# Expert counting for two tiles at a time, and the z chain on 128 rows

## The chip, the cores and the metric

The kernel runs on one core of one Trainium2 chip. Five engines work side by side, each through its own queue in order: TensorE (PE, with its weight loads shown as PEld), VectorE (DVE), ScalarE (ACT), GpSimd (POOL) and SyncE (SP), which here only starts DMAs. The metric is device time in microseconds, lower is better: 367.92 us before the change, the median of 3 runs (367.91 to 368.16).

## The reference

One input x (2048 tokens of 512 numbers) goes through two branches, mixed by a gate:

```python
pq = q @ w_phi; pk = k @ w_phi                       # 32 heads of 16
phi = concat(softmax(p), softmax(-p))                # 32 features a head
kv = sum_s phi_k * v;  z = sum_s phi_k
a = ((phi_q @ kv) / (phi_q @ z + 1e-6)) @ wo         # linear attention
s1, s2 = x @ w_q @ k1, x @ w_q @ k2                  # 32 heads, 16 scores each
e = 16 * argmax(s1) + argmax(s2)                     # one of 256 experts a head
b = sum_h gelu(x @ u[e_h]) * v[e_h]                  # g of a single choice is 1
out = sigmoid(x @ gate_w) * a + (1 - sigmoid(x @ gate_w)) * b
```

The second branch needs, for each token, how many of the 32 heads chose each of the 256 experts: b is (count * gelu(x @ u.T)) @ v.

## The kernel before

The tokens are 16 tiles of 128. Every f32 operand of a large product is split into a high part and a rest (names ending in h and l), and a product takes three matmuls: high by high, high by low, low by high. A first stage builds phi_k, kv and z over all 16 tiles and folds the score weights (tiles sh, sl). The second stage, from L801 on, is a pipeline over tiles that is written out by hand: every engine's queue holds its instructions in the order in which the program issues them. In iteration a it works on tile n = a+1 (scores, L847 to L861, and the choice of the best score, `best`), tile a (attention softmax, `soft_in` to `soft_b`), b = a-1 (phi turned by a DMA transpose, `planes` and `join`; the coefficients, `coef` and `c_planes`), z = a-2 (attention numerator, `mid_num`, and its tile c, `c_join`, `back_cl`) and y = a-3 (output product po, `push` and `pop`, with the rest of the numerator, `num_lo`).

TensorE's order in an iteration is: front_q(a) (bank pq), po(y), the mask of tile a (mk, `mid_mask`), oT(z), the scores s0(n) and s1(n), then pp(n). The 18 matmuls of po(y) are 8 with xh, then 6 with c (the last two with its low part cl), then 4 with xl.

The choice: DVE takes the maximum of 16 scores (L515) and marks the places that equal it (L516, tile eq); when both halves are marked, SP starts a DMA transpose of eq into et (`turn_eq`, L525), and TensorE multiplies et by powers of two in mk (L580): each head's choice becomes one bit in a 16-bit word. This mk stands in PE's queue ahead of the rest of the next iteration.

The counting (`count`, L585) is a chain of 17 small DVE instructions on 16-bit and 32-bit words, in 16 steps: four shifted ORs (L593 to L596), two XORs in one step (L600, L602), an AND into a table X (L613), then the usual bit sums (L616 to L624) and an addition of bytes into cf (L627). It is a generator: `step(t)` issues its next instruction, so its instructions are dealt out between the other work of DVE. Four ORs of tile a go into `soft_b(a)`, the other steps of tile b into the softmax of the next iteration (`dealt`, L785); tile 15, the last, is counted early, one or two steps an iteration. The softmax ends in four short DVE instructions (L494 to L500) and a multiplication on POOL (L507, two halves). POOL also computes w = phi * z (L479), `gelu_in` (L441), `gelu_out` (L451) and `coef` (L631).

The z chain runs once, in iteration 0: z lies in 8 columns; its high and low parts make a tile of 128 x 16 (`z_split`), which is transposed to 16 rows (`z_rows`, L744), multiplied by a selector (L748), and spread to all partitions by two matmuls with 16 rows (`z_spread`, L755).

## Time and profile before

| what | value |
|---|---|
| median of 3 runs | 367.92 us |
| time of the profiled execution | 368.09 us |
| its span, from the first to the last instruction | 366.3 us |
| TensorE busy | 361.1 us, 99% of the span |
| VectorE busy | 313.2 us, 86%, 729 instructions |
| ScalarE busy | 239.7 us, 65% |
| GpSimd busy | 159.9 us, 44% |
| granted TensorE clock | 1.00 |

A row of the timeline reads: start in us from the span's beginning, duration in us, engine, line, operation, output<-input, shapes, and in brackets the idle time before it and what ended it. Consecutive like instructions are merged into one row, and "x2" is their number. Instructions of one engine overlap at their ends, so the distance of two starts, not the duration, is what an instruction costs in a queue that never idles. A group row (out<-in xcount | busy, mean ns of one | idle before) sums all instructions of one line and shape.

### The profile page before, as it was taken

What the parts mean: (1) busy time and instruction counts of PE and PEld (TensorE: products, weight loads), DVE (VectorE), ACT (ScalarE), POOL (GpSimd) and SP (SyncE); (2) the same over time, 40 slices, a digit from 0 to 9 for tenths busy, and PEclk for the clock granted to TensorE, in tenths of its full rate; (3) what the DMA queues carried; (4) which work ended last, traced back from release to release, by engine and by line L of the source; (5) the groups of instructions that cost most, each with busy time, mean ns of one, the idle gap of its engine ahead of it and who ended that gap; (6) DMA issues with size and microseconds to landing.
All of it is one profiled execution on the core that took longest, in us unless ns stands there. A gap on an engine that the chain in (4) does not pass through costs nothing.

```text
span 366.3 us, 8798 instructions
## 1 busy us (share of the span) xinstructions
PE 361.1 (99%) x3512; PEld 289.9 (79%) x3512; DVE 313.2 (86%) x729; ACT 239.7 (65%) x440; POOL 159.9 (44%) x171
## 2 busy tenths in 40 slices
PE   8999999999999999999999999999999999999995
PEld 3767787787777888878888888888888888888874
DVE  2459898866759979989999999999999999999883
ACT  4444557636538555778687596696786876968552
POOL 2204365525323833627245364374363463453730
PEclk9999999999999999999999999999999999999999
DMA  7939987596492017541451433626514524445101
GB/s 267 411 145 369 280 242 239 131 266 229 87 321 31 2 31 104 141 88 25 86 111 44 99 86 74 102 68 91 103 44 108 104 50 87 106 54 103 57 31 57
DMA packets 71673, 46.49 MB, mean 127 GB/s; under 512 B 63184, under 2 KB 63824, under 8 KB 69328
## 3 DMA queue, kind: packets, MB, share of 16 engines
q1 hardware_dynamic: 70768, 45.17, 47.5%
q10 hardware_dynamic: 864, 0.76, 0.7%
q8 instruction: 27, 0.44, 0.5%
q14 instruction: 14, 0.11, 0.1%
...
## 4 chain that ended last, share of the span: by engine, by line
PE 97%; DMA 1%; SPq 0%; DVE 0%; ACT 0%; issue 0%
PE po L673 15%; PE s L62 7%; PE s L63 7%; PE s L61 6%; PE ws L243 4%; PE pq L62 4%; PE pk L63 4%; PE pq L63 4%; PE pk L62 4%; PE pv L63 4%; PE pv L62 3%; PE pk L61 3%; PE pq L61 3%; PE s L59 3%; PE oT L561 3%; PE pv L61 3%
## 5 line engine op out<-in xcount | busy, mean ns | idle before, releaser
L479 POOL TENSOR_TENSOR w<-d,zb 128x512 f32<-128x512 f32 x32 | 40.8, 1294 | 80.5 <-ACT d L473 78.2
L220 POOL TENSOR_TENSOR d<-d,st 128x1024 f32<-128x1024 f32 x16 | 31.1, 1942 | 60.7 <-DVE st L219 60.7
L62 PE MATMUL s<-sl,xh 128*128 128x480 f32 x124 | 46.9, 378 | 0.0
L63 PE MATMUL s<-sh,xl 128*128 128x480 f32 x124 | 46.9, 378 | 0.0
L473 ACT ACTIVATE d<-d 128x512 f32<-128x512 f32 x32 | 20.0, 631 | 39.0 <-DVE d L123 30.5
L507 POOL TENSOR_TENSOR d<-d,st 128x512 f32<-128x512 f32 x30 | 31.3, 1063 | 24.6 <-DVE st L500 21.2
L553 ACT COPY pt<-tp 128x1024 uint16<-128x1024 uint16 x28 | 36.9, 1393 | 0.0
L61 PE MATMUL s<-sh,xh 128*128 128x480 f32 x93 | 35.3, 380 | 0.0
L392 ACT ACTIVATE d<-d 128x1024 f32<-128x1024 f32 x15 | 15.9, 1063 | 28.3 <-DVE d L125 28.3
L542 ACT COPY pl<-d 128x1024 uint16<-128x1024 uint16 x28 | 29.2, 1044 | 3.6 <-POOL d L507 3.6
L63 PEld LDWEIGHTS s<-sh,xl 128*128 128x128 f32 x124 | 23.3, 188 | 3.7
L62 PEld LDWEIGHTS s<-sl,xh 128*128 128x128 f32 x124 | 23.3, 188 | 3.1
L62 PE MATMUL pq<-wal,xh 128*128 128x480 f32 x64 | 24.3, 380 | 0.0
L63 PE MATMUL pk<-wah,xl 128*128 128x480 f32 x64 | 24.3, 380 | 0.0
L63 PE MATMUL pq<-wah,xl 128*128 128x480 f32 x64 | 24.3, 380 | 0.0
L62 PE MATMUL pk<-wal,xh 128*128 128x480 f32 x64 | 24.3, 379 | 0.0
L218 DVE TENSOR_REDUCE st<-d 128x64 f32<-128x1024 f32 x16 | 19.5, 1216 | 4.8 <-ACT d L392 4.5
L516 DVE TENSOR_TENSOR eq<-s,mx 128x512 bf16<-128x512 f32 x32 | 22.1, 692 | 1.1
L483 DVE TENSOR_REDUCE st<-d 128x32 f32<-128x512 f32 x32 | 21.5, 681 | 1.7 <-ACT d L473 0.5
L487 DVE TENSOR_REDUCE st<-w 128x32 f32<-128x512 f32 x32 | 20.6, 677 | 2.2 <-POOL w L479 2.2
L63 PE MATMUL pv<-wbh,xl 128*128 128x512 f32 x56 | 22.0, 393 | 0.0
L62 PE MATMUL pv<-wbl,xh 128*128 128x512 f32 x56 | 21.9, 391 | 0.0
...
## 6 DMA issues: line engine op xcount, KB each, us to landing
...
```

The lines of the kernel that those rows point to most:

```text
L61: pe.matmul(o_, ah, bh[:, r], start=False, stop=False)
L62: pe.matmul(o_, ah, bl[:, r], start=False, stop=False)
L63: pe.matmul(o_, al, bh[:, r], start=False, stop=(last and i == n - 1))
L220: pool.tensor_tensor(g64(d), g64(d), b64(st[:, 128:192]), op=ALU.mult)
L479: pool.tensor_tensor(hs(e["w"], i), hs(e["ph"], i), hs(zb, i), op=ALU.mult)
L483: dve.tensor_reduce(pair(e["st"][:, 64:128])[:, :, 1 - i], hs(e["ph"], i), axis=AX.X, op=ALU.add)
L487: dve.tensor_reduce(pair(e["st"][:, 128:192])[:, :, i], hs(e["w"], i), axis=AX.X, op=ALU.add)
L507: eng.tensor_tensor(g64(d)[:, gs_], g64(d)[:, gs_], r[:, gs_].unsqueeze(2).to_broadcast([P, 32, F]), op=ALU.mult)
L516: dve.tensor_tensor(e["eq"][:, 512 * half:512 * half + 512].rearrange("p (h f) -> p h f", f=F), p3, mx.unsqueeze(2).to_broadcast([P, H, F] ...
L542: act.copy(pl, e["ph"][:, halves[i]].bitcast(U16).rearrange("p (c j) -> p j c", j=2))
L553: act.copy(p16[:, :, 4 * i:4 * i + 4, :], e["tp"][i].rearrange("p (j g) n -> p j g n", j=2))
L673: pe.matmul(h["po"], lhs(), rhs, start=first, stop=last)
```

## The change

Tiles are put into groups: (0, 1), (2, 15), (3, 4), (5, 6), (7, 8), (9, 10), (11, 12), and 13 and 14 alone. The word tables sa and sb hold two tiles side by side. When the mask of a group's later tile is there, one chain counts for both tiles, with operands twice as wide; it is dealt out by `tick(tag)`, which is called at named places of the iteration and issues as many steps as two tables say: `deal_a` for a chain begun in this iteration (9 steps, from the end of the softmax to the end of `best(n, 1)` and behind it), `deal_b` for one begun in the iteration before (7 steps, from `num_lo` on). So a chain begins in every second iteration: 1, 2 (tiles 2 and 15), 4, 6, 8, 10, 12, then 13 and 14 on single tiles. For the earlier tile of a pair (0, 3, 5, 7, 9, 11) the coefficients, their transpose, `c_join` and `back_cl` come an iteration later than before, at other places of the queues of POOL, ACT, SP and DVE.

The z chain: zc becomes 128 x 128 (zeros beyond its 16 columns, set by POOL), so that the transpose, the selector's multiplication and the two spreading matmuls run with 128 rows. Further, ch and cl share one tile c, and in the last iterations `gelu_pre(last)` moves behind `mid_num(z)` on ACT.

The diff, cut to its core:

```diff
@@ -403,12 +402,25 @@
     zb = w2.tile([P, 1024], F32, name="zb", bufs=1)
-    chains = {}
+    chains, group = {}, {}
+    for g in [(0, 1), (2, NT - 1), (3, 4), (5, 6), (7, 8), (9, 10), (11, 12), (13,), (14,)]:
+        for i, t in enumerate(g):
+            group[t] = g, i if len(g) == 2 else t % 2 ^ 1
+    early = (0, 3, 5, 7, 9, 11)
 
...
                 del chains[t]
+
+    deal_a = dict(y0=1,y1=1,q0=1,q1=1,q2=1,q3=1,q4=1, m1=1, e1=1)
+    deal_b = dict(x0=1, x1=1, mx=1, mn=2, d0=2)
+    now = [0]
+
+    def tick(tag):
+        t = now[0]
+        step(t - 1, deal_b.get(tag, 0))
+        step(t, deal_a.get(tag, 0))
 
@@ -481,26 +493,28 @@
         dve.tensor_reduce(pair(e["st"][:, 64:128])[:, :, 1 - i], hs(e["ph"], i), axis=AX.X, op=ALU.add)
+        tick(f"s{i}")
 
...
         dve.tensor_reduce(pair(e["st"][:, 128:192])[:, :, i], hs(e["w"], i), axis=AX.X, op=ALU.add)
-
-    def soft_b(t, step=step):
+        tick(f"y{i}")
+
+    def soft_b(t, tick=tick):
         e = st8[t]
...
         sm, y, n_ = st[:, 64:128], st[:, 128:192], st[:, 192:224]
-        step(t)
+        tick("q0")
         dve.tensor_tensor(y, y, sm, op=ALU.mult)
-        step(t)
+        tick("q1")
         dve.tensor_tensor(n_, pair(y)[:, :, 0], pair(y)[:, :, 1], op=ALU.add)
-        step(t)
+        tick("q2")
         dve.reciprocal(n_, n_)
-        step(t)
+        tick("q3")
         dve.scalar_tensor_tensor(pair(y), pair(sm), e["g"][:, 2:3], n_.unsqueeze(2).to_broadcast([P, H, 2]),
...
         r = y
-        step(t)
+        tick("q4")
         for i, s_ in enumerate(halves):
@@ -513,13 +527,14 @@
         dve.tensor_reduce(mx, p3, axis=AX.X, op=ALU.max)
+        tick(f"m{half}")
         dve.tensor_tensor(e["eq"][:, 512 * half:512 * half + 512].rearrange("p (h f) -> p h f", f=F), p3,
...
         if t == NT - 1:
-            e["et"] = w4.tile([P, 8, P], BF16, tag="last", bufs=1, name=f"et{t}")
+            e["et"] = w4.tile([P, 8, P], BF16, tag="c", name=f"et{t}")
         else:
@@ -570,6 +585,7 @@
             dve.tensor_tensor(k2(ol), o[q][:, :2 * P], k2(oh), op=ALU.subtract)
+            tick(f"x{q}")
 
@@ -579,52 +595,58 @@
                               wm[:, q, :], start=(q == 0), stop=(q == 1))
-        chains[t] = count(t, o)
-        next(chains[t])
-
...
+        g, i = group[t]
+        act.copy(sa[:, :, i, :, 8:24], o.rearrange("p (h w a) -> p h w a", w=2, a=F))
+        if t == g[0] == 2 or (t == g[-1] and g[0] != 2):
+            chains[t] = count(g, i)
+
+    def count(g, i):
+        n = len(g)
+        ts = slice(0, 2) if n == 2 else slice(i, i + 1)
+        A, B = (l[:, :, ts].rearrange("p h t w a -> p (h t w) a") if n == 2 else l[:, :, i] for l in (sa, sb))
+        part = lambda l, c: l[:, :, c] if n == 2 else l[:, :, :, c]
         bor = ALU.bitwise_or
...
+        for d, (O, I) in zip((1, 2, 4, 8), ((B, A), (A, B), (B, A), (A, B))):
+            yield dve.tensor_tensor(part(O, slice(8, 24)), part(I, slice(8, 24)), part(I, slice(8 - d, 24 - d)), op=bor)
+        m1 = w3.tile([P, 2, 32, 2], U16, tag="m1", bufs=1, name=f"m1{g[0]}")[:, :n]
+        m2 = w3.tile([P, 2, 32], U16, tag="m2", bufs=1, name=f"m2{g[0]}")[:, :n]
+        row = lambda h, c: sa[:, h, ts, :, c].rearrange("p t w a -> p (t w) a")
+        now, past = slice(8, 24), slice(7, 23)
+        twice = lambda a: a.unsqueeze(3).to_broadcast([P, 2 * n, F, 2])
+        dve.tensor_tensor(m1.rearrange("p t (w a) j -> p (t w) a j", a=F), twice(row(0, now)), twice(row(0, past)),
                           op=ALU.bitwise_xor)
...
+        yield dve.tensor_tensor(m2.rearrange("p t (w a) -> p (t w) a", a=F), row(1, now), row(1, past),
                                 op=ALU.bitwise_xor)
...
+        X = w3.tile([P, 2, 2 * NX], U16, tag="X", bufs=1, name=f"X{g[0]}")[:, :n]
+        T = w3.tile([P, 2, 2 * NX], U16, tag="T", bufs=1, name=f"T{g[0]}")[:, :n]
+        Xf, Tf = (a.rearrange("p t n -> p (t n)") for a in (X, T))
+        x32, t32 = Xf.bitcast(U32), Tf.bitcast(U32)
         srl, band = ALU.logical_shift_right, ALU.bitwise_and
...
+        m1w = m1.rearrange("p t a b -> p (t a b)").bitcast(U32).rearrange("p (w a) -> p w a", a=F)
+        m2w = m2.rearrange("p t a -> p (t a)").bitcast(U32).rearrange("p (w b) -> p w b", b=8)
+        yield dve.tensor_tensor(x32.rearrange("p (w a b) -> p w a b", a=F, b=8),
+                                m1w.unsqueeze(3).to_broadcast([P, 2 * n, F, 8]),
+                                m2w.unsqueeze(2).to_broadcast([P, 2 * n, F, 8]), op=band)
         yield dve.tensor_scalar(t32, x32, 1, 0x55555555, op0=srl, op1=band)
...
+        yield dve.tensor_tensor(Xf, Xf, Tf, op=ALU.subtract)
         yield dve.tensor_scalar(t32, x32, 2, 0x33333333, op0=srl, op1=band)
         yield dve.tensor_single_scalar(x32, x32, 0x33333333, op=band)
...
+        yield dve.tensor_tensor(Xf, Xf, Tf, op=ALU.add)
+        h, q = n * NX, n * NX // 2
+        yield dve.tensor_tensor(Tf[:, :h].rearrange("p (t n) -> p t n", n=NX), X[:, :, :NX], X[:, :, NX:], op=ALU.add)
+        yield dve.tensor_scalar(x32[:, :q], t32[:, :q], 4, 0x0F0F0F0F, op0=srl, op1=band)
+        yield dve.tensor_single_scalar(t32[:, :q], t32[:, :q], 0x0F0F0F0F, op=band)
+        yield dve.tensor_tensor(Xf[:, :h], Xf[:, :h], Tf[:, :h], op=ALU.add)
+        x8 = Xf[:, :h].bitcast(U8).rearrange("p (n b) -> p n b", b=2)
+        cf = w3.tile([P, 2 * NX], F32, tag="cf", bufs=1, name=f"cf{g[0]}")
+        outs = [cf[:, :NX], cf[:, NX:]] if g[-1] != NT - 1 else [cf[:, :NX], w4.tile([P, NX], F32, name="C15", bufs=1)]
+        for t, c in zip(g, outs):
+            st8[t]["C"] = c
+        if g[-1] == NT - 1:
+            for c, k in zip(outs, (slice(0, NX), slice(NX, 2 * NX))):
+                yield dve.tensor_tensor(c, x8[:, k, 0], x8[:, k, 1], op=ALU.add)
+        else:
+            yield dve.tensor_tensor(cf[:, :h], x8[:, :, 0], x8[:, :, 1], op=ALU.add)
 
...
@@ -737,16 +761,16 @@
         act.copy(zc[:, :8], acc[:, :, F])
-        dve.tensor_tensor(zc[:, 8:], acc[:, :, F], zc[:, :8], op=ALU.subtract)
+        dve.tensor_tensor(zc[:, 8:16], acc[:, :, F], zc[:, :8], op=ALU.subtract)
 
...
         o = mm_bank("zT")
-        pe.transpose(o[:16, :P], zc.bitcast(F32), ident)
-        zm = w2.tile([P, 1024], F32R, tag="w", bufs=1, name="zm")[:16].rearrange("p (g n) -> p g n", n=P)
+        pe.transpose(o[:, :P], zc.bitcast(F32), ident)
+        zm = w2.tile([P, 1024], F32R, tag="w", bufs=1, name="zm").rearrange("p (g n) -> p g n", n=P)
         for j in range(2):
             js = slice(4 * j, 4 * j + 4)
-            dve.tensor_tensor(zm[:, js], o[:16, :P].unsqueeze(1).to_broadcast([16, 4, P]),
-                              cs[:16, 160:168][:, js].unsqueeze(2).to_broadcast([16, 4, P]), op=ALU.mult)
+            dve.tensor_tensor(zm[:, js], o[:, :P].unsqueeze(1).to_broadcast([P, 4, P]),
+                              cs[:, 160:168][:, js].unsqueeze(2).to_broadcast([P, 4, P]), op=ALU.mult)
         return zm
@@ -761,16 +785,15 @@
     rawo = {}
-    one = w2.tile([16, P], F32R, name="one", bufs=1)
-    act.copy(one, ones[:16].to_broadcast([16, P]))
+    one = w2.tile([P, P], F32R, name="one", bufs=1)
+    act.copy(one, ones.to_broadcast([P, P]))
+    zc = w2.tile([P, P], F32R, tag="zc", bufs=1, name="zc")
+    pool.memset(zc.bitcast(F32), 0.0)
     best(0, 0)
...
     w4 = ctx.enter_context(tc_pool("w4", "right"))
-    for l in (sa, sb):
-        l.append(w4.tile([P, 4, 24], U16, tag=f"s{len(sa)}{len(sb)}", bufs=1, name=f"s{len(sa)}{len(sb)}"))
-        pool.memset(l[2], 0)
     turn_eq(0)
@@ -785,27 +808,26 @@
             for _ in gate(a):
-                step(b)
-            step(b, 4)
-            if z >= 0:
+                pass
+            tick("mx")
+
+        def second():
+            tick("mn")
+            if z >= 0 and z not in early:
                 back_cl(z)
 
-        def second():
-            step(b, 5)
-            if 2 < a:
-                step(last, 2 if a < 6 else 1)
-
-        moves = iter((first, second, lambda: step(b, 2), lambda: None))
+        moves = iter((first, second, lambda: tick("d0"), lambda: tick("d1")))
         return lambda: next(moves)()
...
         n, b, z, y = a + 1, a - 1, a - 2, a - 3
+        now[0] = a
         B, Z, Y = b >= 0, z >= 0, y >= 0
...
             planes(b, 0)
-            if Z:
+            if Z and z not in early:
                 c_join(z)
@@ -822,15 +844,21 @@
             num_lo(y)
+        else:
+            tick("x0")
+            tick("x1")
         if B:
             soft_in(a, dealt(a, b, z))
-            drain(b)
+            if Z and z in early:
+                coef(z)
         else:
...
             soft_exp(a)
+        if Z and z in early:
+            c_planes(z)
         if a == 2:
@@ -878,8 +906,11 @@
             gelu_out(b)
-            coef(b)
-            c_planes(b)
+            if b not in early:
+                coef(b)
+                c_planes(b)
+            if Z and z in early:
+                c_join(z)
         if a == 1:
@@ -888,15 +919,20 @@
         turn_eq(n)
+        if Z and z in early:
+            back_cl(z)
+        tick("e1")
+        if B:
+            drain(b)
         if a == 0:
...
         if a == 5:
-            neg = w2.tile([P, P], F32R, name="neg", bufs=1)
+            neg = w2.tile([P, P], F32R, tag="zc", name="neg", bufs=1)
             act.activation(neg, ident, AF.Copy, scale=-1.0)
-        if a == 2:
-            step(last, 2)
     a, b, z = NT - 2, NT - 3, NT - 4
+    now[0] = a
+    deal_b = dict(x0=1, x1=1, mx=1, mn=2, d0=2, d1=1)
     planes(b, 0)
@@ -909,11 +945,11 @@
     gelu_act(a)
-    gelu_pre(last)
     push(z - 1, True, own["pp"])
...
     mid_num(z)
+    gelu_pre(last)
     join(b, 0)
@@ -955,7 +991,7 @@
     gelu_out(a)
-    soft_b(last, lambda t: None)
+    soft_b(last, lambda tag: None)
     push(a)
```

The order of two pieces is shown as the program issues it; names are those of tiles, with the number of their buffer. First VectorE at the end of iteration 2, from the softmax of tile 2 (tile st) over the choice for tile 3 (its second half of scores is s_3, the marks are eq) to the first of the two rests of the numerator (xl); sa, sb, m, X and T belong to the counting. Before:

```order
L494 TENSOR_TENSOR st_2107<-st_2107 128x64
L593 TENSOR_TENSOR sb_82<-sa_80 128x4x16
L496 TENSOR_TENSOR st_2107<-st_2107 128x32
L594 TENSOR_TENSOR sa_80<-sb_82 128x4x16
L498 RECIPROCAL st_2107<-st_2107 128x32
L595 TENSOR_TENSOR sb_82<-sa_80 128x4x16
L500 SCALAR_TENSOR_TENSOR st_2107<-st_2107,gs_1977 128x64
L596 TENSOR_TENSOR sa_80<-sb_82 128x4x16
L515 TENSOR_REDUCE mx_3_2258<-s_3_2198 128x32
L516 TENSOR_TENSOR eq_2233<-s_3_2198,mx_3_2258 128x512
L593 TENSOR_TENSOR s_1587<-s_1585 128x4x16
L572 TENSOR_TENSOR xl<-oT_0_2178,xh 128x256
```

And now, behind the four ORs (L610):

```order
L616 TENSOR_TENSOR m_2223<-sa 128x128
L618 TENSOR_TENSOR m_2224<-sa 128x64
L512 RECIPROCAL st_2081<-st_2081 128x32
L627 TENSOR_TENSOR X_2228<-m_2223,m_2224 128x512
L514 SCALAR_TENSOR_TENSOR st_2081<-st_2081,gs_1954 128x64
L630 TENSOR_SCALAR T_2229<-X_2228 128x512
L529 TENSOR_REDUCE mx_3_2235<-s_3_2163 128x32
L631 TENSOR_TENSOR X_2228<-X_2228,T_2229 128x1024
L531 TENSOR_TENSOR eq_2198<-s_3_2163,mx_3_2235 128x512
L686 TENSOR_TENSOR c_2217<-ctj_2215,c_2217 128x256
L632 TENSOR_SCALAR T_2229<-X_2228 128x512
L587 TENSOR_TENSOR xl<-oT_0_2143,xh 128x256
```

The four ORs (128x8x16 now) begin between the two sums of w (L487 before, L500 now), earlier by two places; five further instructions of the chain (L616, L618, L627, L630, L631) now stand ahead of the second comparison (L531), and the rest of tile 0's coefficients (L686) and one more step (L632) between it and xl.

Second, VectorE in the softmax of the last tile, from its sums to the weights. Before:

```order
L483 TENSOR_REDUCE st_4607<-d_4606 128x32 x2
L487 TENSOR_REDUCE st_4607<-w_4676 128x32 x2
L494 TENSOR_TENSOR st_4607<-st_4607 128x64
L496 TENSOR_TENSOR st_4607<-st_4607 128x32
L498 RECIPROCAL st_4607<-st_4607 128x32
```

And now:

```order
L495 TENSOR_REDUCE st_4445<-d_4444 128x32 x2
L500 TENSOR_REDUCE st_4445<-w_4513 128x32
L631 TENSOR_TENSOR X_4435<-X_4435,T_4436 128x512
L500 TENSOR_REDUCE st_4445<-w_4513 128x32
L632 TENSOR_SCALAR T_4436<-X_4435 128x256
L508 TENSOR_TENSOR st_4445<-st_4445 128x64
L510 TENSOR_TENSOR st_4445<-st_4445 128x32
```

A step of tile 14's chain (L631, L632) now follows each of the two sums of w, ahead of the four short instructions. On TensorE the order is the same in both programs; only the shape of zT changes.

More of the change, by code (lines that the diff above doesn't have):

```diff
@@ L78, in mix_kernel @@
     ones = per.tile([P, 1], F32, name="ones")
-    zc = per.tile([P, 16], F32R, name="zc")
     cs = per.tile([P, 168], F32, name="cs")
@@ L84, in mix_kernel @@
     wd = per.tile([P, NK, 32], F32, name="wd")
-    sa = [per.tile([P, 4, 24], U16, name=f"sa{i}") for i in range(2)]
-    sb = [per.tile([P, 4, 24], U16, name=f"sb{i}") for i in range(2)]
+    sa = per.tile([P, 2, 2, 2, 24], U16, name="sa")
+    sb = per.tile([P, 2, 2, 2, 24], U16, name="sb")
     def xs(t, k):
@@ L298, in mix_kernel @@
         pe.matmul(wps[:, :384], warm[:, 1:P + 1], warm, start=True, stop=True)
-    for a in sa + sb:
+    for a in (sa, sb):
         pool.memset(a, 0)
@@ L581, in mid_mask @@
                               wm[:, q, :], start=(q == 0), stop=(q == 1))
-        chains[t] = count(t, o)
-        next(chains[t])
-    def count(t, o):
-        e = st8[t]
-        i = 2 if t == NT - 1 else t % 2
-        A, B = sa[i], sb[i]
-        bor = ALU.bitwise_or
-        act.copy(A[:, :, 8:24], o.rearrange("p (g a) -> p g a", a=F))
-        yield True
-        yield True
-        yield dve.tensor_tensor(B[:, :, 8:24], A[:, :, 8:24], A[:, :, 7:23], op=bor)
-        yield dve.tensor_tensor(A[:, :, 8:24], B[:, :, 8:24], B[:, :, 6:22], op=bor)
-        yield dve.tensor_tensor(B[:, :, 8:24], A[:, :, 8:24], A[:, :, 4:20], op=bor)
-        yield dve.tensor_tensor(A[:, :, 8:24], B[:, :, 8:24], B[:, :, 0:16], op=bor)
-        m1 = w3.tile([P, 32, 2], U16, tag="m1", name=f"m1{t}")
-        m2 = w3.tile([P, 32], U16, tag="m2", name=f"m2{t}")
-        twice = lambda a: a.unsqueeze(3).to_broadcast([P, 2, F, 2])
-        dve.tensor_tensor(m1.rearrange("p (w a) j -> p w a j", a=F), twice(A[:, 0:2, 8:24]), twice(A[:, 0:2, 7:23]),
+        g, i = group[t]
@@ L601, in count @@
                           op=ALU.bitwise_xor)
-        yield dve.tensor_tensor(m2.rearrange("p (w a) -> p w a", a=F), A[:, 2:4, 8:24], A[:, 2:4, 7:23],
+        yield dve.tensor_tensor(m2.rearrange("p t (w a) -> p (t w) a", a=F), row(1, now), row(1, past),
                                 op=ALU.bitwise_xor)
-        if t == NT - 1:
-            X, T = (e["et"].rearrange("p a n -> p (a n)").bitcast(U16)[:, 512 * i:512 * i + 512] for i in range(2))
-        else:
-            X = w3.tile([P, 2 * NX], U16, tag="X", bufs=1, name=f"X{t}")
-            T = w3.tile([P, 2 * NX], U16, tag="T", bufs=1, name=f"T{t}")
@@ L623, in count @@
-        yield dve.tensor_single_scalar(t32[:, :NX // 2], t32[:, :NX // 2], 0x0F0F0F0F, op=band)
-        yield dve.tensor_tensor(X[:, :NX], X[:, :NX], T[:, :NX], op=ALU.add)
-        e["C"] = T.bitcast(F32) if t == NT - 1 else w3.tile([P, NX], F32, tag="cf", name=f"cf{t}")
-        x8 = X[:, :NX].bitcast(U8).rearrange("p (n b) -> p n b", b=2)
-        yield dve.tensor_tensor(e["C"], x8[:, :, 0], x8[:, :, 1], op=ALU.add)
+        yield dve.tensor_tensor(Xf, Xf, Tf, op=ALU.add)
+        h, q = n * NX, n * NX // 2
@@ L638, in c_planes, with c_tile @@
         sp.dma_start_transpose(e["tc"], pl.rearrange("p j c -> p (j c)"))
+    def c_tile(t):
+        c = w4.tile([P, 2, 2 * P], F32R, tag="c", name=f"c{t}")
+        return c[:, 0], c[:, 1]
     def c_join(t):
@@ L644, in c_join @@
                  e["tc"].rearrange("p (j k) n -> p j k n", j=2))
-        ch = w4.tile([P, 2 * P], F32R, tag="ch", name=f"ch{t}")
-        cl = w4.tile([P, 2 * P], F32R, tag="cl", name=f"cl{t}")
+        ch, cl = c_tile(t)
         act.copy(ch, tj)
@@ L654, in back_c @@
                       is_transpose=True, skip_group_check=True)
-        ch = w4.tile([P, 2 * P], F32R, tag="ch", name=f"ch{t}")
-        cl = w4.tile([P, 2 * P], F32R, tag="cl", name=f"cl{t}")
+        ch, cl = c_tile(t)
         act.copy(ch, o[:, :2 * P])
```

10 lines of the change are left out of this document (removed).

## The prediction

> **What bounds the kernel now.** I read the page's first and fourth parts, then the waits of TensorE, then a stretch of one iteration's length (from the middle of iteration 5).
>
> ```profile
> span 366.3 us, 8798 instructions
> PE 361.1 (99%) x3512; PEld 289.9 (79%) x3512; DVE 313.2 (86%) x729; ACT 239.7 (65%) x440; POOL 159.9 (44%) x171
> PE 97%; DMA 1%; SPq 0%; DVE 0%; ACT 0%; issue 0%
> PE warm L298 <- POOL tab L284: 1.2, 1, 1.2
> 205.90:220.30 14.40, 14.40 (x108) 12.11 (x106) 13.85 (x40) 10.69 (x22) 6.79 (x7) 1.00 0.36 81
> ```
>
> TensorE works 361.1 of 366.3 us, it is 97% of the chain that ends last, and the only wait of note is 1.2 us at the start. In the stretch (columns: length, then PE, PEld, DVE, ACT, POOL, granted clock 1.00) it is full, while VectorE has 13.85 of 14.40 us to do and still makes nobody wait. So shorter counting on VectorE gains nothing by itself. The time changes only where TensorE gets less to do, or where something reaches it later. What reaches it last is the mask: VectorE marks the second score half (eq), SP starts the transpose, TensorE wants et for mk. Three rows each of iterations 3 and 6:
>
> ```profile
> 172.50 1.23 SPq L525 DMA_TRANSPOSE et<-eq  x1
> 175.18 1.08 PE L673 MATMUL po<-wbh,xl 128*128 128x512 f32 x4
> 176.10 0.36 PE L580 MATMUL mk<-wm,et 128*128 128x16 bf16 x8
> ...
> 216.66 1.23 SPq L525 DMA_TRANSPOSE et<-eq  x1
> 218.43 1.08 PE L673 MATMUL po<-wbh,xl 128*128 128x512 f32 x4
> 219.43 0.36 PE L580 MATMUL mk<-wm,et 128*128 128x16 bf16 x8
> ```
>
> The matmuls ahead of mk need (175.18 to 176.10) 0.92 us from the start of their row. In iteration 6 mk comes 1.00 after, 0.08 late: there it waited for et, 219.43 − 216.66 = **2.77 us** after the issue, the price from issue to mask. In iteration 3 mk starts at 176.10, so the issue was needed at 173.33 and came at 172.50: a reserve of 0.83 us. Two reserves further on will be worked out the same way. The prediction is a comparison of these reserves with what is put ahead of eq.
>
> **The z chain.** The spreading matmuls with 16 rows (L755) stand among score products:
>
> ```profile
> 131.41 0.38 PE L63 MATMUL s<-sh,xl 128*128 128x480 f32 x1
> 131.72 0.73 PE L755 MATMUL z<-zm,one 16*128 16x512 f32 x2
> 132.38 0.50 PE L59 MATMUL s<-sh,xh 128*128 128x512 f32 x1
> 132.72 0.38 PE L62 MATMUL s<-sl,xh 128*128 128x480 f32 x1
> ```
>
> From 131.41 to 132.72 four matmuls took 1.31 us. With 128 rows a stream of 512 costs (1.08 − 0.38) / 3 = 0.23 by the row of four at 175.18, one of 480 proportionally 0.22: 0.22 + 3 × 0.23 = 0.91. Gain: **−0.40**, at least 0 (if the extra time isn't from the rows), at most −0.45. The larger multiplication by the selector, the memset of zc and the copy of one lie beside the score products and cost nothing, since z is ready for L755 behind other matmuls; without that cover the memset alone, shorter than the 1.04 us of a POOL half (below), would be seen.
>
> **Fewer instructions on VectorE.** 692 become 584; pairs save VectorE about 2.6 us in two iterations (16 steps less, at 0.1 to 0.25 of fixed cost each, by the rows below). It removes the 0.08 at iteration 6: **−0.07**.
>
> **What the wide steps cost ahead of eq.** The rows by form (last: sum, mean ns of one, idle time before):
>
> ```profile
> L617 DVE TENSOR_TENSOR X<-X,T 128x512 uint16<-128x512 uint16 x15 | 6.4, 425 | 0.5
> L624 DVE TENSOR_TENSOR X<-X,T 128x256 uint16<-128x256 uint16 x15 | 4.2, 283 | 0.0
> L593 DVE TENSOR_TENSOR sb<-sa 128x64 uint16<-128x64 uint16 x15 | 2.8, 190 | 0.0
> L616 DVE TENSOR_SCALAR T<-X 128x256 uint32<-128x256 uint32 x15 | 4.4, 295 | 0.5
> L622 DVE TENSOR_SCALAR X<-T 128x128 uint32<-128x128 uint32 x15 | 3.4, 227 | 0.5
> ```
>
> 256 elements more cost 425 − 283 = 142 ns, so the subtraction of 1024 takes 425 + 2 × 142 = 0.71; a shift of 512 takes 295 + 2 × 68 = 0.43. The AND of 512 u32 is priced as the subtraction, 0.71 (the same number of bytes; between 0.43 and 0.85, twice L617); the two XORs (128 and 64 elements) at 0.4 together, L593's 0.19 and a little more. Together 2.25 us, all new ahead of the second comparison.
>
> **Iteration 2, for mk(3).** VectorE and POOL before:
>
> ```profile
> 167.56 1.27 DVE L487 TENSOR_REDUCE st<-w 128x32 f32<-128x512 f32 x2
> 168.86 0.65 DVE L494 TENSOR_TENSOR st<-st 128x64 f32<-128x64 f32 x1
> 169.55 0.74 DVE L496 TENSOR_TENSOR st<-st 128x32 f32<-128x32 f32 x1
> 170.22 0.18 DVE L594 TENSOR_TENSOR sa<-sb 128x64 uint16<-128x64 uint16 x1
> 171.74 0.69 DVE L516 TENSOR_TENSOR eq<-s,mx 128x512 bf16<-128x512 f32 x1
> ...
> 168.69 0.73 POOL L451 TENSOR_TENSOR px<-x,px 128x256 f32<-128x256 f32 x1
> 169.51 0.74 POOL L631 TENSOR_TENSOR cf<-cf,px 128x256 f32<-128x256 f32 x1
> 171.08 2.08 POOL L507 TENSOR_TENSOR d<-d,st 128x512 f32<-128x512 f32 x2 [0.83 <-DVE st L500]
> ```
>
> L494 on 64 numbers takes 0.65 us and ends at 169.51, just behind px (169.42); L496 on 32 numbers takes 0.74 and ends with cf. Both have two inputs in SBUF, and each ends when the POOL operation ends that was running. [...]
>
> The ORs have two SBUF inputs as well. They now begin behind the first L487, at about 168.2, in the middle of the same POOL work, so the third is free where L594 was, at 170.2. From L594's start to eq's end (172.43) it was 2.21 us; the chain then adds 2.25. Of the rest, L494 and L496 (now L508, L510) come behind the hold, +0.24, against two ORs that now lie in it, −0.24. So eq ends at 170.22 + 2.21 + 2.25 = 174.68 and the issue, 0.07 behind, is at 174.75. Needed: 173.33. mk(3) is **1.4 us late**. Behind eq on VectorE stand tile 0's cl (L686), a step and xl; they end some 0.7 and 1.0 behind their need in po, which is inside the 1.4, because po stands ahead of mk.
>
> Ends: without any hold the two waits (0.40 + 0.51 over L494's 0.25 and L496's 0.23) would be missing, 174.75 − 0.9 − 173.33 = +0.5. If the wide subtraction is held by the second half of d (2.08 / 2 = 1.04), +2.5.
>
> **Iteration 13, for mk(14).** The chain of tile 13 has single width, but the same nine steps stand ahead of eq.
>
> ```profile
> 326.46 1.27 DVE L487 TENSOR_REDUCE st<-w 128x32 f32<-128x512 f32 x2
> 328.64 0.28 DVE L500 SCALAR_TENSOR_TENSOR st<-st,gs 128x64 f32<-128x64 f32 x1
> 329.00 2.08 POOL L507 TENSOR_TENSOR d<-d,st 128x512 f32<-128x512 f32 x2 [1.61 <-DVE st L500]
> 329.66 0.69 DVE L516 TENSOR_TENSOR eq<-s,mx 128x512 bf16<-128x512 f32 x1
> 330.43 1.23 SPq L525 DMA_TRANSPOSE et<-eq  x1
> 334.23 0.36 PE L580 MATMUL mk<-wm,et 128*128 128x16 bf16 x8
> ```
>
> Reserve: 334.23 − 2.77 − 330.43 = 1.03. New ahead of eq: two XORs 0.25, AND 0.43, shift 0.29, subtraction 0.43, about 1.3 with gaps. VectorE comes to this place earlier by what the pair of iteration 12 leaves, 0 to 0.6. The subtraction stands 0.33 + 0.72 behind L500's successor, just where d's first half ends (0.36 + 1.04 behind L500's start): if the second half goes first, 1.04 more. So −0.3 to +1.3; I take **+0.4**.
>
> **The softmax of the last tile.** Two steps, a subtraction (0.43) and a shift (0.29), stand ahead of its weights.
>
> ```profile
> 353.46 1.29 DVE L507 TENSOR_TENSOR d<-d,st 128x512 f32<-128x512 f32 x2
> 354.48 1.05 PE L533 MATMUL pt<-cs,d 128*128 128x128 f32 x8
> ```
>
> The first half of d ends 354.1, the second 354.75; TensorE starts on the first at 354.48 and, after four of eight, on the second at about 354.9. Of the 0.5 that the two steps add beyond idle time, 0.3 to 0.4 is reserve for the first and 0.15 for the second: **+0.3**, between 0 and +0.7.
>
> **The pairs in between** (iterations 4, 6, 8, 10, 12; the steps stand ahead of eq of tile a + 1), by iteration 6's example:
>
> ```profile
> 222.80 0.38 PE L63 MATMUL s<-sh,xl 128*128 128x480 f32 x1
> 225.73 0.68 DVE L515 TENSOR_REDUCE mx<-s 128x32 f32<-128x512 f32 x1
> 230.25 0.69 DVE L516 TENSOR_TENSOR eq<-s,mx 128x512 bf16<-128x512 f32 x1
> 233.84 0.36 PE L580 MATMUL mk<-wm,et 128*128 128x16 bf16 x8
> ```
>
> The first maximum can start when the last matmul of its scores is out, about 0.4 behind 222.80, at 223.21, instead of 225.73, since VectorE no longer comes late from the steps of the iteration before: −2.52. Then the 2.25: eq ends at 230.94 − 2.52 + 2.25 = 230.67, the issue is at 230.74, needed at 233.84 − 2.77 = 231.07. Reserve 0.33, so **0**; an OR held by px as in iteration 2 would take it. In the odd iterations no step stands between the sums of w and eq.
>
> **Sum.** −0.40 − 0.07 + 1.4 + 0.4 + 0.3 = +1.6. The profiled execution took 368.09 (span 366.3 and 1.8 around it), 0.17 above the median; I add to the median: 367.92 + 1.6 = 369.5.
>
> **Rivals.**
> A: the time that VectorE saves covers all three places; only z and the 0.07 remain: 367.92 − 0.47 = 367.45. For it: VectorE has 0.5 us of idle time in an iteration, and POOL's px and cf need not lie where they lay. Against: in iteration 2 no pair has yet saved anything, and 2.25 against 0.83.
> B: the pairs in between stall too. The wide subtraction comes to d's boundary there (shift 0.43 and maximum 0.72 behind L514, against the 0.36 + 1.04 from L500's start to the end of d's first half, so at nearly the same moment) and waits for the second half: 1.04 − 0.33 = 0.7 each, five times: 369.5 + 3.5 = 373.0. It decides from 0.33 us of hold on. For it: L494 and L496 show such holds, L494's ending where px ends. Against: no row shows an instruction of VectorE that waited through both halves, and cf, which held in iteration 2, is moved away in these iterations.
> C: the other side from z alone, that is, more than the 0.45 or an earlier first stage: 367.0. Nothing speaks for it but the unknown price of 128 rows.
>
> **How the numbers follow.** Forecast (stalls at the three places, 368.5 to 371.5) 0.47, A 0.23, B 0.23, C 0.07. Less than 0.2% (0.74 us) can't be told from no change here. Slower takes the forecast and B, less 0.03 for stalls that z nearly pays: 0.67; A and these: 0.26; C: 0.07. The range from A's 367.4 to 372.6, most of the way to B, leaves out C and half of B; the forecast's own goes from 0.5 + 0.1 + 0.3 − 0.4 to 2.5 + 1.3 + 0.3 − 0.4, rounded.
>
> **What would show it.** z: the four matmuls take 0.91. Iteration 2: L531's second row ends near 174.7 (less z's 0.4), TensorE waits over 1 us for et at mk(3), and the waits of TensorE name it. Iteration 13: a wait at mk(14) under 1.3. Tail: pt waits for d. B shows as waits at mk(5), (7), (9), (11), (13). Wrong if TensorE shows no wait at mk(3): then the ORs weren't held or the steps are cheaper than their rows.

## The result and the profile after

The changed kernel takes 371.76 us (median of 6 runs, 371.47 to 373.63), the kernel before beside it 367.98 (6 runs, 367.83 to 368.43): ratio 1.0114, 95% interval 1.0091 to 1.0136 (it goes by all runs; two of the six, 373.07 and 373.63, lift it above the 1.0103 of the medians). It is slower by 3.8 us, about 1%. The profiled execution has a span of 369.95 us, 3.64 more than before. Its page, first and fourth part, and TensorE's own waits (us in total, times, longest):

```profile
span 370.0 us, 8685 instructions
PE 362.6 (98%) x3512; PEld 290.2 (78%) x3512; DVE 304.5 (82%) x611; ACT 239.0 (65%) x440; POOL 165.0 (45%) x168
PE 67%; DVE 18%; ACT 6%; DMA 6%; issue 1%; SPq 0%; ACTq 0%; DVEq 0%
PE mk L596 <- DMA et<-eq: 1.1, 2, 0.6
PE po L697 <- DVE xl L587: 0.5, 1, 0.5
PE po L697 <- DVE c L686: 0.3, 1, 0.3
```

VectorE got what was meant: 118 instructions and 8.7 us of work less. TensorE, whose order is unchanged, lost time: the chain that ends last, 97% TensorE before, now runs for 18% through VectorE and 6% through DMAs, and there are new waits for et, xl and c.

Since both programs issue the same 3512 matmuls in the same order, the start of each can be subtracted from that of its counterpart. The difference steps up at few places: +0.47 in the first 10 us (loads of the first stage; in the eleven experiments below, which share this start, it lies between −0.2 and +0.5, so it is scatter), −0.31 at z, **+2.30** between po and mk in iteration 3, −0.07 at mk(6), +0.26 at mk(7), +0.27 at mk(13), **+0.67** at mk(14), and next to nothing behind it (pt, in the softmax of the last tile, starts 0.24 later, of which 0.22 comes back): 3.6 in all. Iteration 3 and the choice ahead of it:

```profile
168.41 0.68 DVE L610 TENSOR_TENSOR sb<-sa 128x128 uint16<-128x128 uint16 x1
169.62 0.21 DVE L610 TENSOR_TENSOR sa<-sb 128x128 uint16<-128x128 uint16 x1
169.86 0.74 DVE L610 TENSOR_TENSOR sb<-sa 128x128 uint16<-128x128 uint16 x1
173.16 0.95 DVE L631 TENSOR_TENSOR X<-X,T 128x1024 uint16<-128x1024 uint16 x1
174.03 0.68 DVE L531 TENSOR_TENSOR eq<-s,mx 128x512 bf16<-128x512 f32 x1
175.24 0.95 DVE L632 TENSOR_SCALAR T<-X 128x512 uint32<-128x512 uint32 x1
176.11 0.41 DVE L587 TENSOR_TENSOR xl<-oT,xh 128x256 fp32r<-128x256 f32 x1
...
166.36 2.64 POOL L901 TENSOR_TENSOR wbl<-rawo,wbh 128x512 fp32r<-128x512 f32 x2 [1.37 <-ACT wbh L867]
169.79 0.73 POOL L653 TENSOR_TENSOR cf<-cf,px 128x256 f32<-128x256 f32 x1
172.38 2.65 POOL L521 TENSOR_TENSOR d<-d,st 128x512 f32<-128x512 f32 x2 [1.86 <-DVE st L514]
174.99 0.91 POOL L453 TENSOR_TENSOR x<-x,px 128x256 f32<-128x256 f32 x1
...
174.78 1.23 SPq L540 DMA_TRANSPOSE et<-eq  x1
176.57 1.40 PE L697 MATMUL po<-wbh,xl 128*128 128x512 f32 x4 [0.47 <-DVE xl L587]
178.57 0.36 PE L596 MATMUL mk<-wm,et 128*128 128x16 bf16 x8 [0.59 <-DMA et<-eq]
```

Of four ORs of equal size two take 0.7 us: the first ends with wbl (169.0), the third with cf (170.5). The issue of et is at 174.78, and mk, which stood at 176.10, starts at 178.57. The shift L632 takes 0.95 us beside x on GpSimd. That shift has one input in SBUF, and the same shape is quick elsewhere; the groups by form (sum, mean ns, idle time before) set L630 against L632 and L631 against the later sum L634:

```profile
L630 DVE TENSOR_SCALAR T<-X 128x512 uint32<-128x512 uint32 x7 | 2.9, 411 | 0.0
L632 DVE TENSOR_SCALAR T<-X 128x512 uint32<-128x512 uint32 x7 | 4.8, 681 | 0.0
L631 DVE TENSOR_TENSOR X<-X,T 128x1024 uint16<-128x1024 uint16 x7 | 6.4, 911 | 0.0
L634 DVE TENSOR_TENSOR X<-X,T 128x1024 uint16<-128x1024 uint16 x7 | 4.7, 677 | 0.0
```

A second thing changed that the prediction didn't have. Issue to mask was 2.77 us before; now it is 236.54 − 233.34 = 3.20 at mk(7) and 337.86 − 334.60 = 3.26 at mk(14):

```profile
233.34 1.23 SPq L540 DMA_TRANSPOSE et<-eq  x1
236.54 0.36 PE L596 MATMUL mk<-wm,et 128*128 128x16 bf16 x8
334.60 1.23 SPq L540 DMA_TRANSPOSE et<-eq  x1
337.86 0.36 PE L596 MATMUL mk<-wm,et 128*128 128x16 bf16 x8 [0.51 <-DMA et<-eq]
```

The profile's list of DMA issues (count, median us from issue to landing) says it for all of them. Before:

```profile
tp<-pl SPq DMA_TRANSPOSE x28, 3.3
et<-eq SPq DMA_TRANSPOSE x16, 2.8
```

After:

```profile
tp<-pl SPq DMA_TRANSPOSE x28, 2.8
et<-eq SPq DMA_TRANSPOSE x16, 3.2
```

The two transposes have swapped their pace, though neither was edited. Each moves 1024 packets of 256 bytes; the packets of an undisturbed transfer span 1.08 us for et and 1.41 for tp before, and the other way round after. What differs is where the source tiles start in a partition: the new tile sizes moved eq from a multiple of 256 bytes to 192 behind one, and pl, the source of tp, from 64 behind one to a multiple. No trace by itself shows that the place sets the pace; two experiments test it.

### The profile page after: what moved, and what is told of

Its sections match the earlier page's. It is cut to its first block, busy times and chain, and to the rows that moved or that the text cites. A ratio compares the mean times of both kernels' runs of the same rounds, so it can differ in the third digit from the quotient of the medians.

```text
span 370.0 us, 8685 instructions
## 1 busy us (share of the span) xinstructions
PE 362.6 (98%) x3512; PEld 290.2 (78%) x3512; DVE 304.5 (82%) x611; ACT 239.0 (65%) x440; POOL 165.0 (45%) x168
## 4 chain that ended last, share of the span: by engine, by line
PE 67%; DVE 18%; ACT 6%; DMA 6%; issue 1%; SPq 0%; ACTq 0%; DVEq 0%
PE po L697 7%; PE ws L242 4%; PE s L62 4%; PE s L63 4%; PE pk L63 4%; PE pk L62 4%; PE pv L63 3%; PE pv L62 3%; PE s L61 3%; PE pk L61 3%; DMA et<-eq 3%; PE pv L61 3%; DMA tpc<-plc 2%; PE kvacc L226 2%; DVE eq L531 2%; DVE mx L529 2%
## 5 line engine op out<-in xcount | busy, mean ns | idle before, releaser
L521 POOL TENSOR_TENSOR d<-d,st 128x512 f32<-128x512 f32 x30 | 34.8, 1181 | 37.5 <-DVE st L514 35.4
L485 ACT ACTIVATE d<-d 128x512 f32<-128x512 f32 x32 | 19.1, 624 | 11.7 <-DVE d L124 5.9
L653 POOL TENSOR_TENSOR cf<-cf,px 128x256 f32<-128x256 f32 x14 | 10.4, 742 | 35.3 <-DVE cf L649 34.8
L529 DVE TENSOR_REDUCE mx<-s 128x32 f32<-128x512 f32 x32 | 21.8, 682 | 5.2 <-PE s L63 5.2
L531 DVE TENSOR_TENSOR eq<-s,mx 128x512 bf16<-128x512 f32 x32 | 22.0, 688 | 1.2 <-DMA et<-eq 0.4
L500 DVE TENSOR_REDUCE st<-w 128x32 f32<-128x512 f32 x32 | 21.2, 677 | 1.5 <-POOL w L491 1.3
```

What stands on the lines that cost most here:

```text
L500: dve.tensor_reduce(pair(e["st"][:, 128:192])[:, :, i], hs(e["w"], i), axis=AX.X, op=ALU.add)
L521: eng.tensor_tensor(g64(d)[:, gs_], g64(d)[:, gs_], r[:, gs_].unsqueeze(2).to_broadcast([P, 32, F]), op=ALU.mult)
L529: dve.tensor_reduce(mx, p3, axis=AX.X, op=ALU.max)
L531: dve.tensor_tensor(e["eq"][:, 512 * half:512 * half + 512].rearrange("p (h f) -> p h f", f=F), p3, mx.unsqueeze(2).to_broadcast([P, H, F] ...
```

## The experiments

The theory after the result: TensorE waits for et because of (1) where eq starts, and (2) what stands ahead of eq on VectorE, its own length and the time for which GpSimd holds it. Times stand beside the kernel before, run on the same chip (368.2 to 368.4 there).

### Where eq starts: moved in the kernel before, put back in the changed one

```diff
     zb = w2.tile([P, 1024], F32, name="zb", bufs=1)
+    w2.tile([P, 192], U8, name="pad2", bufs=1)     # 64 in the changed kernel
...
     w3 = ctx.enter_context(tc_pool("w3", "left"))
+    w3.tile([P, 64], U8, name="pad3", bufs=1)      # 192 in the changed kernel
```

The kernel before, with eq moved:

> The kernel before with two unused bytes rows put in: 192 bytes a partition ahead of the tile eq and 64 behind it, so that eq starts 192 bytes behind a multiple of 256 (as it does in the changed kernel) in place of 0, and every other transposed tile keeps its place within 256. Theory 1 (the place of eq sets the pace of its transposing DMA: 1.08 us in the records of before, 1.41 in those after): each burst of et takes 1.41, the price from issue to mask rises from 2.77 to about 3.2, TensorE waits at the masks whose reserve is under 0.33 (iterations 4 to 13), and the time becomes 368.3 to 370. Rival (et is slower after the change because of what else is under way at that time, or because it starts after an idle stretch): burst 1.08, time 367.9 to 368.1.

368.63 us against 368.31, ratio 1.0019 (1.0005 to 1.0032). The list of DMA issues now has

```profile
tp<-pl SPq DMA_TRANSPOSE x28, 3.2
et<-eq SPq DMA_TRANSPOSE x16, 3.2
```

so et alone became slower, and nothing else was edited. TensorE loses 0.24 at mk(4) and 0.15 at mk(5), the first masks whose reserve (0.24 and 0.19) is less than what et lost, 0.07 at mk(6), and 0.5 in all. The time is at the lower end of what was expected; that a later TensorE also gives the next choice more time fits this, but is argued.

The changed kernel, with eq put back:

> The changed kernel with 64 unused bytes a partition ahead of eq and 192 behind it, so that eq starts at a multiple of 256 again and the planes of the softmax keep their place. Theory 1: et's bursts take 1.08; the waits at the masks of iterations 7 and 13 (0.26 and 0.27) vanish, those of 3 and 14 shrink by about 0.33 each: 371.76 - 1.2 = 370.6 (370.3 to 370.9). Rival (other transfers or the idle stretch ahead): no change, 371.5 to 372.0.

370.39 us, ratio 1.0058 (1.0046 to 1.0071), 1.4 less than the changed kernel's 371.76 (of which the first 10 us explain 0.65 in the profiles: −0.18 here, +0.47 there). Its row in the list is again

```profile
et<-eq SPq DMA_TRANSPOSE x16, 2.8
```

and the steps at mk(7) and mk(13) are gone, the one in iteration 3 is 1.96 in place of 2.30; the one at mk(14) stays at 0.61, 0.06 less where 0.33 was expected: without the wait at mk(13) TensorE is earlier, and eq's issue comes 1.65 us later against it than in the kernel before, in place of 1.22. Both directions speak for the place of eq, worth about 0.9 us at the masks here (0.26 + 0.27 + 0.34 + 0.06), of which this profile loses 0.2 again at an oT near 343.6 us, as no other run does; the idle stretch ahead or other traffic would not follow two unused strips of memory. Where et itself starts made no difference here: it is 64 bytes behind a multiple of 256 in the kernel before and at a multiple in the changed one, and in both the packets take 1.08 us with eq at a multiple and 1.41 with eq elsewhere.

### The z chain alone

```diff
-    zc = per.tile([P, 16], F32R, name="zc")
...
-        pe.transpose(o[:16, :P], zc.bitcast(F32), ident)
+        pe.transpose(o[:, :P], zc.bitcast(F32), ident)
...
-    one = w2.tile([16, P], F32R, name="one", bufs=1)
+    one = w2.tile([P, P], F32R, name="one", bufs=1)
```

> The kernel before with the z chain on 128 rows alone, and 64 unused bytes ahead of eq so that the transposed tiles start where they do before, within 256. The prediction's term: the four matmuls from 131.41 take 0.91 in place of 1.31, time 367.5 to 367.7. Rival (the span is set elsewhere, or the loads of the first stage take the gain): 367.9 to 368.1.

> The z chain on 128 rows alone with eq in its place, once more, beside the two others. If the 0.3 us that the four matmuls around it save reaches the end, 0.3 below the kernel before; if VectorE's et is what TensorE then waits for (mk(6) waited in the kernel before already), level with it within 0.15.

> The kernel before with the z chain on 128 rows alone and no unused bytes, so that its larger tiles move eq to 192 bytes behind a multiple of 256, as the whole change does. Theory 1: et's bursts take 1.41; z gives 0.3 and the waits at the masks of iterations 4 to 8 take 0.4 to 0.7 as in the kernel with moved eq: 0.1 to 0.5 us above z on 128 rows with eq in its place. Rival (the place of eq hardly matters with this dealing): level with it.

With eq in its place 368.51 against 368.31, and 368.42 against 368.38: ratios 1.0003 (0.9994 to 1.0013) and 1.0008 (0.9990 to 1.0026). The four matmuls do become shorter (first run, 131.73 to 132.75, 1.02 in place of 1.31):

```profile
131.73 0.38 PE L63 MATMUL s<-sh,xl 128*128 128x480 f32 x1
131.94 0.74 PE L755 MATMUL z<-zm,one 128*128 128x512 f32 x2
132.53 0.39 PE L59 MATMUL s<-sh,xh 128*128 128x512 f32 x1
132.75 0.38 PE L62 MATMUL s<-sl,xh 128*128 128x480 f32 x1
```

but the 0.29 does not reach the end, and the expected 367.5 to 367.7 did not come: in the second run TensorE is 0.27 ahead behind z, 0.16 in iteration 3, 0.02 at 348 us and behind by 0.13 at the end, where the products of the last tile start no earlier. Waits for et do not explain it: at no mask does TensorE lose more than 0.01 us in that run. Up to the last tile the lead goes in steps of a few hundredths of a us at most; why stays open. Without the unused strip z's larger tiles move eq, and the kernel takes 368.81, ratio 1.0011 (1.0001 to 1.0021): 0.4 above the median with eq in its place, with steps of 0.33, 0.15 and 0.09 at mk(4), mk(5) and mk(6). The intervals overlap, so it is the steps in the trace that tell the two apart. So the z chain's edit by itself brought the misplaced eq.

### Fewer steps ahead of eq in iteration 2

```diff
+    few_a = dict(q0=1, q1=1, q2=1, q3=1, q4=1)
+    few_b = dict(mx=5, mn=5, d0=2)
...
-        step(t - 1, deal_b.get(tag, 0))
-        step(t, deal_a.get(tag, 0))
+        step(t - 1, (few_b if t == 3 else deal_b).get(tag, 0))
+        step(t, (few_a if t == 2 else deal_a).get(tag, 0))
```

> The changed kernel (eq where the change puts it) with the steps of the chain of tiles 2 and 15 dealt otherwise: the four ORs and the XORs in the softmax of iteration 2, behind both sums of w, and all twelve others in the softmax of iteration 3. Theory (the steps ahead of eq make mk(3) late): the issue in iteration 3 comes at about 173.0 in place of 174.78, TensorE's wait there falls from 2.3 to 0.2 to 0.7, and mk(4) may take up to 0.3: 369.6 to 370.3. Rival (a stall there comes from what POOL and ACT do with tile 0's coefficients one iteration later, so from the pairing, not from the steps): the wait stays above 1.5, 371 to 371.8.

372.01 us, ratio 1.0102 (1.0087 to 1.0118): no gain, and the expectation was wrong twice. The issue came at 173.88, not 173.0:

```profile
171.40 1.08 DVE L620 TENSOR_TENSOR m<-sa 128x64 uint16<-128x64 uint16 x1
171.37 2.08 POOL L523 TENSOR_TENSOR d<-d,st 128x512 f32<-128x512 f32 x2 [1.01 <-DVE st L516]
173.88 1.24 SPq L542 DMA_TRANSPOSE et<-eq  x1
```

The second XOR, 64 small numbers, lasts from 171.40 to 172.48, until d's first half is done (171.37 + 1.04 = 172.41): the last step had been put just behind the instruction that starts d. So the step in iteration 3 is 1.5. And mk(4) takes 1.14: the twelve wide steps in iteration 3 make VectorE late there.

Then the same with the XORs ahead of that instruction:

```diff
-    few_a = dict(q0=1, q1=1, q2=1, q3=1, q4=1)
+    few_a = dict(q0=1, q1=1, q2=1, q3=2)
```

> As the last one (few steps ahead of eq in iteration 2), but with the two XORs one place further ahead, behind the fourth OR and ahead of the instruction that lets GpSimd start on d. Theory 2 (an instruction of VectorE with two inputs in SBUF that comes while GpSimd runs waits for GpSimd's instruction to end; there the second XOR took 1.08 us, to the end of d's first half): both XORs take under 0.3, the issue of et in iteration 3 comes at about 173.0 in place of 173.88, mk(3) is late by 0.3 to 0.7 in place of 1.49: 372.01 - 0.9 = 371.1 (370.8 to 371.4). Rival (the XOR is slow for its own sake, or ahead of something else): it takes 1 us again and the time stays at 371.7 to 372.2.

```profile
171.25 0.19 DVE L620 TENSOR_TENSOR m<-sa 128x64 uint16<-128x64 uint16 x1
173.04 1.23 SPq L542 DMA_TRANSPOSE et<-eq  x1
```

The same XOR takes 0.19 us, the issue is at 173.04 as expected, mk(3) is late by 0.70, at the upper end, with et landing 3.7 us after its issue. The time is 371.44 (ratio 1.0094, 1.0078 to 1.0109), 0.6 less where 0.9 was expected: mk(4) takes 1.52 now, part of what mk(3) gave up.

### Without GpSimd's two multiplications

This kernel leaves out two multiplications of GpSimd for tile 1 in iteration 2.

```diff
-            gelu_out(b)
+            if a != 2:
+                gelu_out(b)
             if b not in early:
-                coef(b)
+                if a != 2:
+                    coef(b)
```

> The changed kernel without two multiplications of GpSimd for tile 1 in iteration 2 (px, the last step of the gelu, and cf, the coefficients times it; the output of tile 1 is then not the reference's). Theory 2: the first OR still waits for wbl (about 0.65), the third takes 0.2 in place of 0.74; et's issue for tile 3 comes 0.5 us earlier and the time is 371.76 - 0.5 = 371.25 (371.0 to 371.5). Rival (the ORs wait for something else): 371.6 to 372.0 and the third OR still over 0.6.

```profile
169.91 0.23 DVE L610 TENSOR_TENSOR sb<-sa 128x128 uint16<-128x128 uint16 x1
174.31 1.23 SPq L540 DMA_TRANSPOSE et<-eq  x1
```

The third OR takes 0.23 in place of 0.74, the first, beside wbl, still 0.69, and the issue is at 174.31, 0.47 earlier; the step in iteration 3 falls from 2.30 to 1.79. The time is 371.03 (ratio 1.0079, 1.0065 to 1.0093), 0.7 less. With the XOR above this shows by two edits, not by coincidence in time alone, that VectorE's instructions with two inputs in SBUF were held by GpSimd's.

### Every tile alone

```diff
-    for g in [(0, 1), (2, NT - 1), (3, 4), (5, 6), (7, 8), (9, 10), (11, 12), (13,), (14,)]:
+    for g in [(0,), (1,), (2, NT - 1)] + [(t,) for t in range(3, 15)]:
...
-    early = (0, 3, 5, 7, 9, 11)
+    early = ()
...
-    deal_b = dict(x0=1, x1=1, mx=1, mn=2, d0=2)
+    deal_b = dict(x0=1, x1=1, mx=1, mn=2, d0=2, d1=1)
```

> The changed kernel with every tile counted alone (2 and 15 excepted), its steps dealt in every iteration by the same two tables with one step more in the second, no coefficients delayed, and eq at a multiple of 256 bytes. What the new dealing costs without the pairs: nine steps of 1.3 us ahead of eq instead of four, but VectorE comes to the maximum earlier by what no longer stands ahead of it, so its sum per iteration is that of before. Theory (only holds and the first chain matter): waits at mk(3) as with pairs (about 2), 0 to 0.3 in other iterations: 369.7 to 371.5. Rival (the earlier placing itself costs in every iteration): 0.5 or more in each of ten iterations, above 373.

369.51 us, ratio 1.0035 (1.0021 to 1.0049), 0.9 below the changed kernel with eq in its place, as it is here too, and a little below the expected 369.7 to 371.5. TensorE loses 0.9 in iteration 3, where about 2 was expected, and 0.7 at mk(4), and nothing at any other mask. The dealing itself costs nothing in the steady iterations; the pairs gain nothing there either.

Nothing is lost at mk(14) either, where the pairs lose 0.61 with eq in its place, though in both kernels the same nine steps of tile 13 stand ahead of eq. The first maximum of tile 14 in iteration 13, with pairs and then with tiles alone:

```profile
326.90 0.68 DVE L530 TENSOR_REDUCE mx<-s 128x32 f32<-128x512 f32 x1
325.75 0.69 DVE L530 TENSOR_REDUCE mx<-s 128x32 f32<-128x512 f32 x1 [0.63 <-PE s L63]
```

Alone, VectorE comes early enough to wait 0.63 us for these scores, and the nine steps still end in time. With pairs the wide steps of tiles 11 and 12 come first in the same iteration; that they are what makes VectorE late is read from the order of its queue, not tested by itself. Iteration 2 is the other place where the steps of a pair, of tiles 0 and 1 there, are followed by a new chain ahead of eq.

### Two dealings that follow from this

Both count 2 and 15 with the ORs and XORs ahead of d, 13 likewise, and have eq in its place. The first puts the last four steps behind eq of tile 4, the second behind xl.

```diff
+    few_a = dict(q0=1, q1=1, q2=1, q3=2)
+    few_b = dict(mx=3, mn=3, d0=2, e1=4)           # without e1 in the second
+    few_c = dict(mx=4, mn=5, d0=2)
-    early = (0, 3, 5, 7, 9, 11)
+    early = (0, 2, 3, 5, 7, 9, 11)
...
             num_lo(y)
+            if a == 4:                              # the second only
+                step(2, 4)
```

> The changed kernel with eq at a multiple of 256 bytes, and the chains of tiles 2 and 15 and of tile 13 dealt as the runs suggest: ORs and XORs ahead of d, no other step ahead of eq; of the chain of 2 and 15 eight steps in the softmax of iteration 3 and four behind eq of tile 4, tile 2's coefficients an iteration later as for the other earlier tiles. Theories 1 and 2 together: waits of 0 to 0.3 at mk(3) and mk(4), up to 0.1 at mk(14), none at the other masks, z 0.3 shorter: 368.0 to 368.5, level with the kernel before at 368.3. Rival (counting for two tiles costs TensorE time that no dealing removes): above 369.5.

369.98 us, ratio 1.0048 (1.0035 to 1.0060): far above what was expected, and within the rival's range, which the second dealing then speaks against. There is no wait at mk(3), mk(13) and mk(14), but one of 0.47 at mk(6) and one of 1.4 for xl, in iteration 4:

```profile
187.91 1.13 DVE L642 TENSOR_SCALAR T<-T 128x256 uint32<-128x256 uint32 x1
190.64 0.75 DVE L591 TENSOR_TENSOR xl<-oT,xh 128x256 fp32r<-128x256 f32 x2
186.81 2.08 POOL L525 TENSOR_TENSOR d<-d,st 128x512 f32<-128x512 f32 x2 [2.49 <-DVE st L518]
191.11 1.20 PE L701 MATMUL po<-wbh,xl 128*128 128x512 f32 x4 [1.23 <-DVE xl L591]
```

A tensor_scalar of 256 numbers, 0.29 elsewhere, takes 1.13, to the end of d (188.89); behind four such steps xl comes at 191. The second dealing:

> The last dealing (fit), but the four last steps of the chain of tiles 2 and 15 not behind eq of tile 4, where xl waited for them and TensorE for xl (1.39 us), but behind xl, in iteration 4. Theory (that stall was VectorE's queue order alone): xl is ready for po(1), the stall goes; mk(4) may wait 0.2, mk(6) 0.47 as in the last run: 369.98 - 1.2 = 368.8 (368.5 to 369.1), 0.1 to 0.2% above the kernel before. Rival (VectorE has no room in iterations 3 and 4 for the pair with tile 15, so the stall comes back at another place): above 369.5.

368.93 us, ratio 1.0015 (0.9999 to 1.0031), as expected: the wait for xl is gone, mk(4) takes 0.19 and mk(6) 0.52. At mk(6) et took 3.6 us from issue to landing. The transposes of two tiles' coefficients, which now stand ahead of et on SyncE in iteration 5, are not enough to explain it, since they stand there at mk(8) as well, where et took 2.8. The DMA view from 216 to 221 us, and from 245 to 250:

```profile
q8 instruction: 1, 0.02, 1.2%
et<-eq SPq DMA_TRANSPOSE x1, 3.6
...
et<-eq SPq DMA_TRANSPOSE x1, 2.8
```

At mk(6) a load of 16 KB of instructions starts 0.8 us behind the issue; at mk(8) there is none. In every kernel with pairs such a load comes behind the issue at mk(6) and mk(12), and et takes 3.3 to 3.8 there; whether the load is the cause is not tested. The second dealing takes back most of the loss; the interval includes no difference. A version clearly below the kernel before is hardly to be had by dealing, since behind its first loads TensorE waits there for some 0.1 us.

## Why the prediction was right, and where not

The sign, the main cause and the range (367.4 to 372.6) held. The time was 2.3 us above the forecast of 369.5, and just above the forecast's own 368.5 to 371.5. In the profiles the change is 3.64 where 1.6 was forecast: 0.9 more in iteration 3, 0.5 at mk(7) and mk(13), 0.3 at mk(14), 0.1 at z, and 0.5 of scatter in the first stage, less 0.3 in the last softmax.

**The first view.** That VectorE's saved work is worth nothing by itself held: the pairs took 8.7 us off VectorE, and with the stalls dealt away (the last dealing) or the tiles counted alone the kernel is no faster. Its count, 692 instructions to 584, was off (729 and 611 in the pages), and its 2.6 us saved for each pair would make 18 for seven; nothing in the sum rested on either. −0.07 at mk(6) was measured as −0.07, by luck: TensorE stood 2.5 us late there, and in the last dealing, where it stood 0.4 late, mk(6) waits 0.52.

**z**, −0.40: the four matmuls gave 0.29, and alone it is not visible in the time.

**Iteration 2 for mk(3)**, +1.4: +2.30. The working up to the issue held closely: 174.75 forecast, 174.78 measured, with the holds where they were put (the first and third OR, 1.0 us together) and the AND and XORs a little quicker. That it agrees so closely is in part luck, since the scatter of the first stage (+0.47) stood against z's gain; TensorE was 0.2 later there, so for it the issue came 1.25 too late (174.78 − 173.33 − 0.2), where 1.4 was forecast. The subtraction met d's boundary and VectorE went first there: L631 took 0.95 in place of 0.68, and d's two halves 2.65 in place of 2.08, so it was GpSimd that paid most. The step that failed is the price from issue to mask, taken as the constant 2.77: it was 3.79. Of the 1.02 between them, 0.32 are eq's place (3.47 with eq put back). About 0.7 remain: with eq in place et still took 3.4 from issue to landing in iteration 3, while with tiles alone it took 2.8. The DMA view of the changed kernel with eq put back, from 173 to 179 us, and at mk(14), from 333 to 338:

```profile
q14 instruction: 1, 0.01, 0.4%
et<-eq SPq DMA_TRANSPOSE x1, 3.4
...
q14 instruction: 1, 0.01, 1.1%
et<-eq SPq DMA_TRANSPOSE x1, 2.7
```

In the five kernels where et was that slow, a load of 8 KB of instructions starts within 0.15 us of the end of et's packets; with tiles alone it lies ahead of them. But such a load alone does not do it: at mk(14) one starts 0.05 us behind the end of et's packets here, and 0.01 behind it with tiles alone, and et lands after 2.7 in both. The cause stays open. The claim that the lateness of xl is covered by mk(3) held only because et was slow: po waited 1.5 us for c and xl, in place of 0.7 and 1.0, since L632 was held by x (0.95); mk could have started at 177.81 by po, came 0.76 later, and with 2.77 from the issue would have had et at 177.55.

**Iteration 13**, +0.4: +0.67. Against TensorE (2.95 behind by then) the issue came 334.60 − 330.43 − 2.95 = 1.22 us later than before, at the upper end of what was priced (1.3 less 0 to 0.6), where the reserve was 1.03; the rest is issue to mask, 0.49 longer. That the nine steps stand ahead of eq is not the whole cause, as the kernel with every tile alone shows. **The last softmax**, +0.3: the wait at pt came much as forecast, 0.24, but 0.22 of it came back behind it, which the working had not looked at.

**The pairs in between**, 0, with B as rival: with eq in its place they cost 0, as forecast; the +0.26 and +0.27 at mk(7) and mk(13) are eq's place, not B's hold. B's price of 0.7 each was not seen: at d's boundary VectorE's waiting instruction went first, and L631 was held for 0.27 (0.95 in place of 0.68). Rival A fell with the wait at mk(3), C with z.

**Holds with one input in SBUF.** The prediction's holds, those of L494 and L496, were of instructions with two inputs in SBUF. Shifts and ANDs with constants, with one, were held as well, though no edit tests it: L632 took 0.68 on the mean against 0.41 for L630, and another tensor_scalar (L642) 1.13 in the first of the two dealings; in the kernel before, where none of those of 256 numbers ran beside GpSimd, none of the 48 took over 0.30. In iteration 3 of the changed kernel L632 was held ahead of xl.

What no part of the prediction considered is that new tile sizes move other tiles, and that the pace of a transposing DMA went with where its source starts (1.08 or 1.41 us for its packets here).
